# A gated linear attention with a sine-squared MLP behind it: state sums off the tensor engine, paired half blocks, and a new order of work

## The chip, the cores and the metric

The kernel runs on one core of one Trainium2 chip. The metric is the device time of one launch in microseconds; before the change the median of 11 runs is 222.42 us (220.28 to 224.2). The engines of the core work beside each other and wait for each other by semaphores: PE (TensorE, matmuls; its weight loads are shown as PEld), DVE (VectorE), ACT (ScalarE), POOL (GpSimd) and SP (SyncE), which here issues most DMAs.

## The reference, cut to what matters

```python
f = 1.0 / (1.0 + np.exp(-f_logit))                 # B, H, S, D = 4, 8, 768, 48
for t in range(S):
    state = f[:, :, t, :, None] * state + np.einsum('bhd,bhe->bhde', k[:, :, t], v[:, :, t])
    y[:, :, t] = np.einsum('bhd,bhde->bhe', q[:, :, t], state)
x = y.transpose(0, 2, 1, 3).reshape(B * S, H * D)  # 3072 tokens, 384 features
h = x @ w_in                                       # w_in is 384 x 2048
s = np.sin(alpha * h)
g = h + s * s / (alpha + 1e-09)
out = g @ w_out                                    # w_out is 2048 x 384
```

All inputs and the output are float32.

## The kernel before

The sequence is cut into six chunks of 128 steps. A chunk c has four batches b, so 512 tokens. Inputs are loaded and prepared in units u of half a chunk (two batches): u = 2c and 2c+1; a unit and batch pair has the number m. The work has these stages; the names are those of the tiles in the profile.

- **load** (line 271): 48 loads of 384 KB, four per unit (f, k, q, v), all on SP's queue in the order of the list LOADS. The MLP's weights come on POOL's queue: w_in in two halves of eight DMAs (line 295), w_out in four (line 305). Each group stands behind a one-element copy on POOL (`seen`, line 287) that waits for one of the loads; W_GATE says for which position in LOADS.
- **pre(u)**: ACT computes Exp and Ln of the gate logits (lines 333 and 336, tiles f and lf). PE forms their running sums with a triangular mask (cs, lines 363 and 366, five matmuls, and one in the last chunk). ACT takes two exponentials of each (Gi and cs, lines 376 and 372). k times Gi goes to POOL or DVE and q times cs to DVE (qk, line 385); gl (line 380) is the decay over the chunk; v is cast into vb by DVE (lines 342 and 343).
- **attend(c, b)**: q and k are transposed by PE (tp, line 420) and copied to SBUF (tr, line 428) in chunks 0 to 3, or transposed by DMA on SP in chunks 4 and 5 (line 426). Then come the score matmuls (aps, line 437), the causal mask on DVE (at, line 440), the part of the output from the old state (y, line 445, "inter") and from the chunk itself (y, line 458), and the eviction into xT (line 465).
- **the state**: except in the last chunk PE forms k^T v (kv, line 473). From chunk 1 on, one matmul of 512 columns with the identity first adds the old state into the same PSUM tile (line 471). DVE then multiplies the sum by the decay (st, line 479).
- **spread(c)**: six small DMAs on SP or POOL put the features in place in xT (line 508).
- **first(c, fb)**: the MLP's first layer for one of 16 blocks of 128 hidden features. Three matmuls make h (line 529), ACT takes the sine (s, line 534), the square is made by POOL, DVE or ACT (s2, shown as s; lines 542 and 540), and DVE adds it to h (g, line 547). The PSUM bank of h is held until g is done. h has three banks; in chunk 0 some blocks use the two banks of the second layer instead (SPARE). In chunk 0 the layer is done in halves of two batches (256 columns), one half block to a bank; later chunks take 512 columns.
- **second(c, t)**: sixteen matmuls over the g tiles (o, line 566), an eviction (osb, line 574) and a store (line 577).

Exp and Ln share one ACT table and the sine needs another, so ACT's work is cut into phases with a table load (line 628) at each change. PHASES lists them: `("pre", [6, 7, 8])` is the preparation of these units, `("sin", 18)` the next 18 sines. The sines run through the blocks of chunk 0, first half, then second half, then chunk 1 and so on.

The order of everything is found by a planner in the kernel (`in_order`), which runs when the program is built. Each operation has a duration for each engine that may do it, its inputs, the ring of buffers that it takes from, and a rank; the planner starts, again and again, the operation with the smallest start time (plus a BIAS where several engines can do it), and ranks decide ties. KIND, RANK, LAG and ATT are offsets to the ranks by kind of operation and chunk. The instructions of an engine then run strictly in the order that came out. Four lists are kept in a given order whatever the planner finds: loads, ACT's table work, h, and cs.

```python
                key = (s + (BIAS[e] if len(o.engs) > 1 else 0), o.rank, s + d)
...
            if not first:
                nc.tensor.matmul(kv, ident, tl["st", c - 1, b], start=True, stop=False, skip_group_check=True)
...
        hb, sb, s2b = buf("o" if spare else "h"), buf("s"), buf("s2")
```

Of the kernel before, what the change touches and what calls it, by code (L numbers as in the profile page):

```python
# [10 lines left out]
F32 = mybir.dt.float32  # L11
# [6 lines left out]
NG = 36  # L18
PE_TR = 4
SPARE = 15  # L20
LOADS = [("k", 0), ("f", 0), ("q", 0), ("v", 0), ("f", 1), ("v", 1), ("q", 1), ("k", 1), ("f", 3),
    ("k", 3), ("f", 2), ("q", 3), ("q", 2), ("f", 5), ("v", 3), ("v", 2), ("k", 2), ("k", 4),
    ("f", 4), ("v", 4), ("q", 4), ("k", 5), ("v", 6), ("q", 5), ("k", 7), ("v", 7), ("f", 6),
    ("v", 5), ("k", 6), ("f", 7), ("q", 6), ("v", 10), ("f", 8), ("q", 7), ("q", 8), ("k", 8),
    ("v", 8), ("k", 11), ("v", 9), ("v", 11), ("f", 11), ("f", 9), ("k", 9), ("q", 10), ("k",
    10), ("q", 9), ("q", 11), ("f", 10)]
W_GATE = [1, 6, 15]
LAG = [389, 183, 51, 210, 208, 289]
ATT = [150, -130, -181, 58, -47, 55]
PHASES = [("pre", [0]), ("pre", [1]), ("sin", 16), ("pre", [2, 3]), ("sin", 15), ("pre", [4, 5]),  # L30
    ("sin", 17), ("pre", [6, 7, 8]), ("sin", 18), ("pre", [9, 10, 11]), ("sin", 46)]
RANK = [-6, 628, -691, -10, 175, 71, 8, 20, -437, -18, -103, -123]
MULS = {"POOL": 1020, "DVE": 750}
KIND = {"v": [147, 9, 46, 75, 127, -2],
        "cs": [-145, -32, -204, -182, -55, -258],
        "kh": [-179, -112, -104, -31, -147, -299],
        "qh": [-145, -50, -132, -383, -199, -136],
        "tp": [-133, -167, -186, -203, -128, -244],
        "tr": [116, 196, 76, 293, 139, 285],
        "a": [-282, -297, -247, -321, -246, -206],  # L40
        "m": [83, 264, 119, 421, 58, 182],
        "y": [-85, 152, 24, 75, 105, 196],
        "i": [81, 10, -86, -217, 109, 54],
        "kv": [148, 97, 59, 86, 61, 178],
        "st": [129, 130, -157, 126, 215, -54],
        "h": [5, -27, 43, 31, -36, -92],
        "sq": [114, 125, 112, 12, 253, 139],
        "g": [-119, 51, -134, 78, 119, -14],
        "ev": [-69, -174, -183, -117, -240, -203]}
SPREAD = {"SP": 1800, "POOL": 1600}  # L50
BIAS = {"ACT": 400, "DVE": 500, "POOL": 500, "SP": -1800}
# [12 lines left out]
class Op:  # L64
    after, line = 0, None
# [11 lines left out]
def in_order(ops, lines):  # L77
# [28 lines left out]
    while left:  # L106
        best = None
        for o in pending:
# [5 lines left out]
            for e, dur in o.engs.items():  # L114
                s = max(t, free[e])
                if o.dma:
                    s = max(s, dma_free[e] - DMA_AHEAD)
                d = dur + (TABLE_LOAD if o.table and o.table != table and table else 0)
                key = (s + (BIAS[e] if len(o.engs) > 1 else 0), o.rank, s + d)
                if best is None or key < best[0]:  # L120
                    best = (key, o, e, s, d)
# [28 lines left out]
def kernel(  # L150
# [60 lines left out]
    def op(rank, engs, emit, deps=(), takes=(), holds=(), table=None, dma=None):  # L211
# [8 lines left out]
        h=N_H, s=3, s2=3, g=NG, o=2, osb=3).items()}  # L220
# [105 lines left out]
    def pre(u, rank):  # L326
        c = u // NU
# [24 lines left out]
        made["v", u] = op(rank + KIND["v"][c] + 2, {DVE: 1300 if u < NU else 1050}, values, deps=[vb_.ready], takes=[vv], holds=[vb_])  # L352
        late = []
        for i in range(2):
# [34 lines left out]
            c_ = op(rank + KIND["cs"][c] + i, {PE: 170 if last else 370}, cs_, deps=[l], takes=[cb], holds=[lf])  # L389
# [7 lines left out]
            made["kh", m] = op(rank + KIND["kh"][c] + i, MULS, km, deps=[gi, kb_.ready], takes=[qkb], holds=[kb_, Gib])  # L397
            made["qh", m] = op(rank + KIND["qh"][c] + i, {DVE: 490}, qm, deps=[g, qb_.ready], takes=[qkb], holds=[qb_, cb])
# [5 lines left out]
    def attend(c, b, rank):  # L404
# [4 lines left out]
        yb, kvb, sb = buf("a"), buf("a"), buf(f"st{b}")  # L409
# [58 lines left out]
        def kv_(e):  # L468
            kv = tl[x, "kv"] = ps_a.tile([P, HP, 2, E], F32, tag="a", name=f"kv_{c}_{b}")
            if not first:  # L470
                nc.tensor.matmul(kv, ident, tl["st", c - 1, b], start=True, stop=False, skip_group_check=True)
            for p in range(HP):
                nc.tensor.matmul(kv[:, p, :, :], qk_b[qkb.place % NQ][:, 0, p, :, :].rearrange("c r e -> c (r e)"),  # L473
                                 v_b[vb.place % NV][:, p, i, :, 0, :],
                                 start=(first and p == 0), stop=True, skip_group_check=True)

        def st_(e):
            t = tl["st", c, b] = st_pool.tile([P, HP, 2, E], BF16, tag=f"s{b}", name=f"st_{c}_{b}")
            nc.vector.tensor_tensor(t, tl[x, "kv"], tl["gl", m].unsqueeze(3).to_broadcast([P, HP, 2, E]),  # L479
                                    Alu.mult)  # L480

        if c < PE_TR:
            kt = op(rank + KIND["tp"][c], {PE: 250}, lambda e: tp_(e, 0), deps=[made["kh", m]], takes=[tpb], holds=[qkb])
            qt = op(rank + KIND["tp"][c], {PE: 250}, lambda e: tp_(e, 1), deps=[made["qh", m], kt], holds=[tpb, qkb])
            tr = op(rank + KIND["tr"][c], {DVE: 640, ACT: 970}, tr_, deps=[qt], takes=[trb], holds=[tpb])
        else:
            tr = op(rank, {SP: 1300}, tr_, deps=[made["kh", m], made["qh", m]], takes=[trb], holds=[qkb], dma=3000)
        a = op(rank + KIND["a"][c], {PE: 400}, a_, deps=[tr], takes=ab + atb, holds=[trb])
        ms = [op(rank + KIND["m"][c], {DVE: 640}, lambda e, r=r: m_(e, r), deps=[a], holds=[ab[r], atb[r]]) for r in range(2)]
        last_ = None  # L490
        if not first:
            last_ = op(rank + KIND["i"][c], {PE: 265}, inter_, deps=[a, made["st", c - 1, b]], takes=[yb], holds=[trb, sold])
        for r in range(2):
            last_ = op(rank + KIND["i"][c], {PE: 350 if first else 240}, lambda e, r=r: intra_(e, r), deps=[ms[r], last_, made["v", u]],
# [165 lines left out]
```

## Time and profile before

| | us |
|---|---|
| median of 11 runs | 222.42 |
| the profiled execution | 222.77 |
| its span, first to last instruction | 221.0 |
| PE busy (weight loads) | 187.4 (116.0) |
| DVE busy | 164.4 |
| ACT busy | 165.1 |
| POOL busy | 99.6 |
| mean granted PE clock | 0.959 |

The rows of the costliest groups that the change touches, with the shapes kept apart (columns: line, engine, operation, output from input with its shape, count, busy us, mean ns of one, idle time of the engine just before them and what ended it):

```profile
L534 ACT ACTIVATE s<-h,al_p 128x512 f32<-128x512 f32 x80 | 53.7, 687 | 18.0 <-PE h L529 16.4
L542 POOL TENSOR_TENSOR s<-s 128x512 f32<-128x512 f32 x45 | 46.6, 1042 | 59.0 <-ACT s L534 50.4 <-DVE at L440 3.3 <-DVE g L547 2.5
...
L479 DVE TENSOR_TENSOR st<-kv,gl 128x512 bf16<-128x512 f32 x20 | 13.3, 685 | 6.9 <-PE kv L473 6.9
...
L542 POOL TENSOR_TENSOR s<-s 128x256 f32<-128x256 f32 x20 | 12.0, 611 | 12.5 <-ACT s L534 8.6 <-DVE s L542 2.5 <-DVE g L547 1.1
...
L628 ACT ACT_TABLE_LOAD x9 | 11.5, 1283 | 0.2
...
L471 PE MATMUL kv<-st,ident 128*128 128x512 bf16 x16 | 6.1, 381 | 0.0
...
L540 ACT ACTIVATE s<-s 128x256 f32<-128x256 f32 x8 | 3.1, 418 | 0.1
L542 DVE TENSOR_TENSOR s<-s 128x256 f32<-128x256 f32 x4 | 2.2, 559 | 1.5 <-ACT s L534 1.5
```

A matmul's mean here is from its issue to its modelled end, so that consecutive ones overlap: three of 512 columns take 0.65 us together, not 3 times 0.38. Squares and sines share the name s, since numbers in names are left out.

### The profile page before, as it was taken

Reading aid. Unit: us, or ns where it says so; the run is one execution under the profiler, and the core shown is the slowest. Engines: PE = TensorE matmul, PEld = TensorE weight load, DVE = VectorE, ACT = ScalarE, POOL = GpSimd, SP = SyncE. Lnnn points to the kernel's source line nnn. Section 1 sums busy time; section 2 is a strip of 40 time slices with the busy share of each in tenths; the row PEclk is TensorE's granted clock in tenths of the full one; section 3 lists DMA queues with packets and bytes.
Section 4 is the critical chain, followed back from the end, with each engine's and each line's share of the span. In section 5 each row is a group of like instructions: output and inputs, shape, how many; then the busy total and the mean of one; then the engine's idle time right before and its main releaser. Section 6 shows DMA issues by size and latency. Waiting matters only on the chain.

```text
span 221.0 us, 4306 instructions
## 1 busy us (share of the span) xinstructions
PE 187.4 (85%) x1513; PEld 116.0 (52%) x1529; DVE 164.4 (74%) x301; ACT 165.1 (75%) x275; POOL 99.6 (45%) x134
## 2 busy tenths in 40 slices
PE   0269656596999898987799999999999999999993
PEld 0157444474776455653465655566665555555561
DVE  7667766568788999895679989567978958778700
ACT  2545946988569879799978888988877887777511
POOL 5721756059244735673733265375364642123300
PEclk9999997559999999999799999999999999999999
DMA  8999999999990999989599998464500101100211
GB/s 133 189 201 188 192 195 198 189 172 196 188 180 19 174 191 194 175 145 225 142 171 198 175 153 164 136 176 95 98 25 34 73 18 39 38 34 36 74 71 71
DMA packets 115125, 29.61 MB, mean 134 GB/s; under 512 B 108720, under 2 KB 114336, under 8 KB 115104
## 3 DMA queue, kind: packets, MB, share of 16 engines
q1 hardware_dynamic: 111648, 26.04, 67.8%
q0 software_dynamic: 3456, 3.30, 9.0%
q8 instruction: 12, 0.20, 0.4%
q14 instruction: 9, 0.07, 0.1%
HBM read 25.17 MB, written 4.72 MB: 135 GB/s over the span
## 4 chain that ended last, share of the span: by engine, by line
PE 60%; ACT 11%; DMA 10%; DVE 6%; SPq 5%; issue 4%; POOL 2%; ACTq 0%
PE o L566 25%; PE h L529 23%; SPq L271 5%; DMA q<-in_q_dram 4%; PE y L458 4%; DMA w_in_bf<-in_moe_w_in_dram 3%; DMA w_out_bf<-in_moe_w_out_dram 3%; ACT f L333 3%; DVE g L547 2%; PE aps L437 2%; PE y L445 2%; ACT Gi L376 2%; ACT L628 2%; POOL w_in_bf L295 2%; ACT s L534 2%
## 5 line engine op out<-in xcount | busy, mean ns | idle before, releaser
L542 POOL TENSOR_TENSOR s<-s 128x512 f32<-128x512 f32 (+1 forms) x65 | 58.5, 909 | 71.5 <-ACT s L534 59.0
L534 ACT ACTIVATE s<-h,al_p 128x512 f32<-128x512 f32 (+1 forms) x112 | 67.7, 627 | 27.5 <-PE h L529 25.0
L529 PE MATMUL h<-xT,w_in_bf 128*128 128x512 bf16 (+1 forms) x320 | 76.9, 356 | 7.3 <-DVE g L547 3.3
L547 DVE SCALAR_TENSOR_TENSOR g<-s,al_r,h 128x512 bf16<-128x512 f32 (+1 forms) x112 | 72.0, 667 | 12.6 <-POOL s L542 10.1
L566 PE MATMUL o<-w_out_bf,g 128*128 128x384 bf16 x384 | 78.4, 330 | 1.2 <-DMA w_out_bf<-in_moe_w_out_dram 1.2
L566 PEld LDWEIGHTS <-g 128*128 128x128 bf16 x384 | 36.5, 99 | 25.7 <-issue 2.0
L529 PEld LDWEIGHTS <-w_in_bf 128*128 128x128 bf16 x336 | 32.4, 100 | 30.1 <-issue 4.2
L440 DVE TENSOR_TENSOR at<-aps,mask 128x512 bf16<-128x512 f32 x48 | 31.5, 685 | 3.5 <-PE aps L437 3.2
L385 POOL TENSOR_TENSOR qk<-k,Gi 128x384 bf16<-128x384 f32 x22 | 21.6, 1000 | 17.9 <-ACT Gi L376 17.8
L540 ACT ACTIVATE s<-s 128x512 f32<-128x512 f32 (+1 forms) x36 | 20.8, 584 | 0.9
L385 DVE TENSOR_TENSOR qk<-q,cs 128x384 bf16<-128x384 f32 x24 | 13.2, 552 | 10.2 <-ACT cs L372 10.0
L363 PE MATMUL cs<-lf,mask 128*128 128x384 bf16 x24 | 9.0, 382 | 12.5 <-ACT lf L336 10.3
L458 PE MATMUL y<-at,vb 128*128 128x128 bf16 x184 | 18.7, 229 | 0.3 <-DVE at L440 0.3
L479 DVE TENSOR_TENSOR st<-kv,gl 128x512 bf16<-128x512 f32 x20 | 13.3, 685 | 6.9 <-PE kv L473 6.9
L420 PE MATMUL tp<-ident,qk 128*128 128x128 bf16 x128 | 12.1, 251 | 4.2 <-POOL qk L385 2.0
L333 ACT ACTIVATE f<-f 128x768 f32<-128x768 f32 x12 | 10.0, 836 | 6.1 <-POOL seen L287 5.1
L458 PEld LDWEIGHTS <-vb 128*128 128x128 bf16 x184 | 13.3, 103 | 2.4 <-issue 0.2
L574 ACT COPY osb<-o 128x384 f32<-128x384 f32 x16 | 7.6, 478 | 9.1 <-PE o L566 8.9
L437 PE MATMUL aps<-tr 64*128 64x128 bf16 x192 | 10.5, 228 | 4.5 <-DVE tr L428 3.2
L376 ACT ACTIVATE Gi<-cs 128x384 f32<-128x384 f32 x24 | 11.6, 484 | 3.4 <-PE cs L366 2.7
L420 PEld LDWEIGHTS <-qk 128*128 128x128 bf16 x128 | 9.9, 113 | 7.7 <-POOL qk L385 3.7
L465 ACT CAST xT<-y 128x512 bf16<-128x512 f32 (+1 forms) x20 | 11.2, 565 | 1.3 <-PE y L458 1.1
(56 smaller groups left out, 171.5 us busy)
## 6 DMA issues: line engine op xcount, KB each, us to landing
k<-in_k_dram SPq DMA_DIRECT2D x12, 384.0 KB, 6.7
f<-in_f_logit_dram SPq DMA_DIRECT2D x12, 384.0 KB, 6.9
q<-in_q_dram SPq DMA_DIRECT2D x12, 384.0 KB, 6.6
v<-in_v_dram SPq DMA_DIRECT2D x12, 384.0 KB, 7.1
out_dram<-osb SPq DMA_DIRECT2D x24, 192.0 KB, 1.9
w_out_bf<-in_moe_w_out_dram POOLq DMA_DIRECT2D x4, 384.0 KB, 7.8
w_in_bf<-in_moe_w_in_dram POOLq DMA_DIRECT2D x8, 128.0 KB, 5.9
w_in_bf<-in_moe_w_in_dram POOLq DMA_DIRECT2D x4, 96.0 KB, 6.6
```

The costliest lines, as they stand in the source:

```text
L333: nc.scalar.activation(out=tl["f", u], in_=tl["f", u], func=Act.Exp, scale=-1.0)
L376: nc.scalar.activation(out=tl["Gi", m], in_=tl["cs", m][:, :H * D], func=Act.Exp)
L385: engine[e].tensor_mul(qk_b[bufs["qk", m].place % NQ][:, "kq".index(n), :, :, :D], tl[n, u][:, i * H:(i + 1) * H, :].rearrange("c (r p) d ...
L420: nc.tensor.transpose(tl[x, "tp"][:, j * HP + p, :], qk_b[qkb.place % NQ][:, j, p, :, :].rearrange("c r e -> c (r e)"), ident)
L440: nc.vector.tensor_mul(tl[x, "at", r], tl[x, "a"][r], mask4)
L458: nc.tensor.matmul(tl[x, "y"][:, blk, :], v_, tl[x, "at", r][:, p, :], start=(first and p == r == 0), stop=(r == 1), skip_group_check=True)
L529: nc.tensor.matmul(h[:, :n], w_in_bf[:, kb, fs], xT[:, kb, ts], start=(kb == 0), stop=(kb == KB - 1))
L534: nc.scalar.activation(out=s[:, :n], in_=tl[x, "h"][:, :n], func=Act.Sin, scale=al_p[:, fb:fb + 1])
L540: nc.scalar.activation(out=s2[:, :n], in_=s[:, :n], func=Act.Square)
L542: engine[e].tensor_mul(s2[:, :n], s[:, :n], s[:, :n])
L547: nc.vector.scalar_tensor_tensor(tl["g", c, fb][:, ts], tl[x, "s2"][:, :n], al_r[:, fb:fb + 1], tl[x, "h"][:, :n], Alu.mult, Alu.add)
L566: nc.tensor.matmul(tl["o", c, t], tl["g", c, fb][:, t * P:(t + 1) * P], w_out_bf[:, fb, :], start=(fb == 0), stop=(fb == FB - 1))
```

## The change

- **State sums.** From chunk 2 on (SUM = 2) the identity matmul is left out. DVE adds kv and the old state into a new SBUF tile `sum` (two buffers), and the product with gl then reads `sum` and runs on POOL or DVE; in the built program all twelve run on POOL.
- **Pairs in chunk 0.** Two half blocks of 256 columns share one PSUM bank and one s tile. Their sines stay separate (each block has its own scale), the square is one operation over 512 columns, and the two additions stay separate. In the built program all 16 squares of chunk 0 run on POOL.
- **Buffers.** g has 44 buffers in place of 36. SPARE goes from 15 half blocks to 5 pairs.
- **Order.** KIND has an offset for each unit instead of each chunk, ON_ACT adds a bias for ACT by kind and unit, and LOADS, W_GATE, LAG, ATT, PHASES, RANK and BIAS have new values. In PHASES the stage of units 6, 7 and 8 becomes units 6 and 7, three sines, and unit 8.

In the built program the counts on the engines change as follows; all others stay.

| | before | after |
|---|---|---|
| PE: identity matmuls, 512 columns | 16 | 4 |
| DVE: st / sum | 20 / 0 | 8 / 12 |
| POOL: st | 0 | 12 |
| squares of 256 columns, POOL / ACT / DVE | 20 / 8 / 4 | 0 / 0 / 0 |
| squares of 512 columns, POOL / ACT / DVE | 45 / 28 / 7 | 63 / 26 / 7 |
| k products, POOL / DVE | 22 / 2 | 20 / 4 |
| evictions osb, ACT / DVE | 16 / 8 | 10 / 14 |
| copies tr, ACT / DVE | 9 / 7 | 10 / 6 |
| evictions xT, ACT / DVE | 20 / 4 | 18 / 6 |
| ACT table loads | 10 | 12 |

The diff, cut to its core:

```diff
-NG = 36
+NG = 44
-SPARE = 15
+SUM = 2
+SPARE = 5
-W_GATE = [1, 6, 15]
-PHASES = [("pre", [0]), ("pre", [1]), ("sin", 16), ("pre", [2, 3]), ("sin", 15), ("pre", [4, 5]),
-    ("sin", 17), ("pre", [6, 7, 8]), ("sin", 18), ("pre", [9, 10, 11]), ("sin", 46)]
+LOADS = [("v", 0), ("f", 0), ("q", 0), ("k", 0), ("f", 1), ("v", 1), ("q", 1), ("k", 1), ("v", 2),
+    ("f", 2), ("f", 3), ("k", 3), ("q", 2), ("q", 3), ("f", 5), ("v", 3), ("k", 2), ("q", 5),
+    ("q", 4), ("v", 4), ("f", 4), ("k", 4), ("v", 6), ("f", 6), ("k", 5), ("k", 6), ("v", 5),
...
+W_GATE = [5, 5, 18]
+PHASES = [("pre", [0]), ("pre", [1]), ("sin", 16), ("pre", [2, 3]), ("sin", 16), ("pre", [4, 5]),
+    ("sin", 13), ("pre", [6, 7]), ("sin", 3), ("pre", [8]), ("sin", 19), ("pre", [9, 10, 11]),
+    ("sin", 45)]
...
-                key = (s + (BIAS[e] if len(o.engs) > 1 else 0), o.rank, s + d)
+                key = (s + (BIAS[e] + (o.on_act if e == "ACT" else 0) if len(o.engs) > 1 else 0), o.rank, s + d)
...
         def kv_(e):
...
-            if not first:
+            if not first and c < SUM:
                 nc.tensor.matmul(kv, ident, tl["st", c - 1, b], start=True, stop=False, skip_group_check=True)
...
+        def sum_(e):
+            t = tl[x, "sum"] = at_pool.tile([P, HP, 2, E], F32, tag="sum", bufs=2, name=f"sum_{c}_{b}")
+            nc.vector.tensor_tensor(t, tl[x, "kv"], tl["st", c - 1, b], Alu.add)
...
-            nc.vector.tensor_tensor(t, tl[x, "kv"], tl["gl", m].unsqueeze(3).to_broadcast([P, HP, 2, E]),
-                                    Alu.mult)
+            engine[e].tensor_tensor(t, tl[x, "kv"] if c < SUM else tl[x, "sum"],
+                                    tl["gl", m].unsqueeze(3).to_broadcast([P, HP, 2, E]), Alu.mult)
...
+                su = op(rank + KIND["st"][u] + 1, {DVE: 640}, sum_, deps=[kv, sold_op], holds=[sumb, kvb, sold])
+                made["st", c, b] = op(rank + KIND["st"][u] + 1, {POOL: 1040, DVE: 917}, st_, deps=[su, made["gl", m]],
+                                      holds=[sb, sumb, bufs["gl", m]])
...
-    def first(c, fb, ts, rank, needs):
+    def first(c, fbs, ts, rank, needs):
...
+        part = [slice(i * n, (i + 1) * n) for i in range(len(fbs))]
+
+        def mm(e, i):
             pool_, tag = (ps_o, "o") if spare else (ps_h, "h")
...
+                nc.tensor.matmul(tl[x, "h"][:, part[i]], w_in_bf[:, kb, fbs[i] * P:(fbs[i] + 1) * P],
+                                 tl["xT", c][:, kb, ts], start=(kb == 0), stop=(kb == KB - 1))
...
+                engine[e].tensor_mul(s2, s, s)
...
-            for fb in range(FB):
-                sins.append(first(0, fb, HALF[half], 16 * half - 32 + fb, needs(half, fb)))
+            for fb in range(0, FB, 2):
+                sins += first(0, (fb, fb + 1), HALF[half], 16 * half - 32 + fb, needs(half, fb))
```

## The prediction

> **What bounds the kernel now.** I read, in this order and shown so, the page's slices, the windows by stage, the list of waits, ScalarE's timeline at its table loads, and the chain of waits.
>
> ```profile
> PE   0269656596999898987799999999999999999993
> ...
> PEclk9999997559999999999799999999999999999999
> ...
> 75.00:97.40 22.40, 20.59 (x183) 12.26 (x184) 21.32 (x36) 17.96 (x28) 11.88 (x12) 1.00 1.14 184
> 97.40:111.00 13.60, 9.83 (x78) 5.42 (x78) 8.73 (x22) 13.26 (x23) 8.05 (x10) 0.87 0.77 168
> 111.00:135.00 24.00, 23.84 (x209) 14.40 (x209) 21.51 (x36) 20.10 (x33) 10.15 (x12) 1.00 1.17 176
> 135.00:153.00 18.00, 17.89 (x144) 10.93 (x145) 12.69 (x24) 16.58 (x28) 9.79 (x10) 1.00 0.51 130
> 153.00:207.00 54.00, 53.68 (x366) 29.43 (x370) 43.06 (x63) 42.24 (x68) 20.26 (x20) 1.00 0.18 49
> ...
> ACT s L534 <- PE h L529: 25.0, 45, 2.0
> ...
> 97.44 1.28 ACT L628 ACT_TABLE_LOAD   x1
> ...
> 109.49 1.28 ACT L628 ACT_TABLE_LOAD   x1
> 110.79 1.84 ACT L534 ACTIVATE s<-h,al_p 128x512 f32<-128x512 f32 x3
> ...
> 135.59 1.28 ACT L628 ACT_TABLE_LOAD   x1
> ...
> 115.59 0.38 PE h L529
> ...
> 192.09 0.65 PE h L529 x3
> ...
> 207.00 10.41 PE o L566 x64
> ```
>
> In a window line the figures after the length are the busy us of PE, its weight loads, DVE, ACT and POOL, then clock, DMA share, GB/s. ScalarE's sines wait 25.0 us in 45 waits for h. From 111 on PE is busy throughout; before that other engines pace it (DVE 21.3 of 22.4 in chunk 1's first layer; ACT 13.3 of 13.6 in the exp stage from 97.4, where PE loses 3.8). A busy PE hides pipelining, so I count places on PE instead: 0.216 us per 512 columns (three in 0.65), 0.1625 for an o matmul (64 in 10.41), 0.056 for 128 columns (tp, eight in 0.45), 0.041 for one of the paired aps (eight in 0.33), 0.33 for a cs of five. Summed over the instruction list this is 170.9 us. PE ends at 217.4, so 46.5 us are idle or at half clock, nearly all before 115. From block 3 of chunk 2 (115.6) there are 100.9 us of places for 101.8 us. Earlier, every PE wait is repaid; later, only less PE work or a new wait counts.
>
> **What the Trainium skill says.** "TensorE: Matmul & The Clock Gate", section "Wait — 56ns, not 53.3ns?", gives 215.7 ns and 55.6 ns for 512 and 128 columns on a warm array; the trace agrees (0.216, 0.056). Its section "What's actually happening" halves the clock after an idle window: here the granted clock was 0.50 from 40 to 48 us. "ScalarE: Activation LUTs", section "What ACT_TABLE_LOAD costs", gives 1283 ns and a further drain of some 1380. The trace has 1283, and the next activation 0.02 us later, so I use 1.3. "SBUF — State Buffer", section "Who interferes with whom", says that a DVE operation with one SBUF input does not contend with GpSimd, one with two does. The new sum reads one SBUF and one PSUM operand, so it should run like st (684 ns); the casts of v do get blocked (one took 2.72 us at 72.36).
>
> **The change part by part.** The built program's order says what stands where.
>
> 1. Identity matmuls: 12 of 16 go (chunks 2 to 4), 12 × 0.216 = 2.6 us of PE; total 168.3.
>
> 2. The states of these chunks: each st on DVE (0.685) becomes a sum on DVE, taken at 0.685, and a product on POOL, taken at the square's 1.04 since shape and operands are alike (bounds 0.7 and 1.5, as the trace has no broadcast factor on POOL). DVE +0, POOL +12.5. The state is ready some 1.3 us later (1.04 and a hand-over of about 0.2). Behind it stand the next chunk's inter matmuls, which follow after 18 us of PE places or more, so I charge nothing; without that cover each would stall PE by up to 1.3. On POOL the squares and k products queued behind wait up to 1.04; POOL is busy 45%.
>
> 3. Pairs in chunk 0: 32 half squares become 16 full ones. All go to POOL: 16 × 1.04 = 16.7 for 20 × 0.61 before, and 8 × 0.42 = 3.3 us leave ACT, 4 × 0.56 = 2.2 DVE. With two half blocks per bank, six rather than two of the second half's blocks run on PE during the exp stage that starts at 37.9.
>
> 4. Weights and loads: both halves of w_in now follow the sixth load. SP's issues go by about 2.05 us apart and the seventh load landed at 21.2 with 4.3 us of w_in ahead of it, so the sixth lands near 15. The second half of before took 10.1 us from first issue (21.47) to use (31.58); so the first half lands near 25.4 instead of before 21.5, and 16 issues hold POOL for 8.2 us. One tr also moves ahead of the table load. The first sine starts near 28.4 (24.5 before). But before ScalarE then waited twice for h, 2.0 and 1.9 us, the first for w_in's second half; I let both vanish. w_out follows the nineteenth load and POOL's squares, issued about 56 to 63 instead of 48.3 to 54.2; o starts only near 62, so I charge nothing; a landing after 68 would hold cs and cost 1 us per us. On SP the first transpose of chunk 4 now stands ahead of nine loads: nine × 2.05 = 18.5 us after about 111, for first use near 136; free unless 5 us late.
>
> 5. ACT's path. To the first Exp of the stage at 64.9, ACT work falls from 43.9 to 40.7 us (same unit durations for both); with fewer waits I put the first sine of chunk 1 at 71.1, 3.7 earlier than 74.9. Block 0 to block 12: PE places 17.9 instead of 16.5, so 18.1 us becomes 19.5; the sine of block 12 ends at 91.2 (93.5 before). From there to the end of chunk 2's first sine ACT has 21.0 us instead of 16.7: pre of units 6 to 8 is split around three sines, which adds two table loads (2.6), squares and evictions. With the 1.2 us of waits seen before: 91.2 + 22.2 = 113.4 (111.4 before).
>
> 6. Block 3 of chunk 2 needs the bank of block 0: square 1.04, g 0.74, hand-overs 0.3: 115.5, as good as before (115.6). But behind that point stand 94.9 us of PE work instead of 100.9: 1.3 from identity matmuls, 4.7 from output matmuls and others now done in the split stage. That is the gain: 6.0.
>
> 7. What is late next: the last exp stage (units 9 to 11). It now opens after chunk 3's block 2 (before: after block 1, at 135.59, with the next sine at 149.19). Block 6 needs the bank of block 3, so the stage, then sine 3, square and g: 16.5 us after block 2 (0.9 to the table load, 13.0 for the stage without the eviction in it, 0.65, 1.15, 0.8). Between the two PE has 12.9 us of work; before, from block 1 to block 5, it had 17 us of places for 17.6 us. PE starves 3.6 us.
>
> 8. Chunk 4: all 16 squares on POOL, 16 × 1.04 = 16.7 for 21.1 us of PE; a bank turns in about 3.7 us, three banks give 1.23 per block against PE's 1.32. Free, with little to spare: at 4.4 us per turn, 0.15 × 16 = 2.4 us.
>
> Sum: 115.5 + 18.9 (to the end of block 2) + 0.3 + 16.5 + 63.1 + 0.6 = 214.9, and the last eviction and store 3.6: span 218.5 against 221.0. The profiled execution took 222.77, 1.77 more than its span; so 220.3, and as it lies 0.35 above the median of the runs, 219.9.
>
> **The rivals.**
>
> Larger gain: the front gains more, or the starved stage finds PE behind, so the 3.6 of step 7 vanish. For it: 46.5 us of slack to win. Against it: the pacing there is ACT's, in order. 219.9 − 3.6 = 216.3.
>
> No gain: step 6's gain is given back, 3.6 in step 7 and 2.4 in step 8. −6.0 + 6.0 leaves 222.4. For it: POOL's square of one block is the longest link; against: POOL idles 33.7 of 54 us from 153 to 207.
>
> Slower: the front comes later instead of earlier because w_in is late. Place: the first sine of chunk 0. The end follows the sine of block 12 one for one: 219.9 + (t − 91.2). If the 3.9 us of late start are made up only by half, t is 95.5 and the time 224.2. It is slower by over 0.5% from t = 94.8. For it: ACT's path from there is 4.3 us longer, and two table loads cannot be hidden once ACT paces; against: 3.3 us of squares leave ACT.
>
> That the sums do not shorten PE can't be: the 12 matmuls are gone from the list; but their worth is only the 1.3 to 2.6 of step 1.
>
> **How the numbers follow.** Forecast 0.42, larger gain 0.22, no gain 0.14, slower 0.22. A measurement here tells 0.5% (1.1 us) from no change. So faster 0.64, same 0.14, slower 0.22. The likeliest alone spans 217.5 to 221.3. Steps 7 and 8 at their worst with the late front reach 225.5; the larger gain with the front earlier by a further 2.5 reaches 213.8.
>
> **What would show it.** Right: chunk 1's first sine near 71, chunk 2's first table load to sine at 113, block 3 of chunk 2 near 115.5, an idle PE of 3 to 4 us inside the last exp stage, POOL products near 1.04, sums near 0.685. Wrong: the first sine of chunk 0 after 29, cs waiting for w_out, h waiting for POOL's squares in chunk 4, or loads of unit 9 landing after the last exp stage opens.

## The result and the profile after

| | before | after |
|---|---|---|
| median of the runs, us | 222.81 (47 runs, the first 11 among them, 220.11 to 225.47) | 225.89 (12 runs, 224.04 to 227.29) |
| ratio after / before | | 1.0171, 95% interval 1.0136 to 1.0206 |
| profiled execution, us | 222.77 | 224.48 |
| its span, us | 221.0 | 222.7 |
| sine of block 12 of chunk 1 ends | 93.5 | 91.4 |
| h of block 3 of chunk 2 starts on PE | 115.6 | 119.08 |
| PE goes on with chunk 3 in the last exponential stage | no gap | 154.86 |

The change costs 1.7% by the ratio; the medians differ by 3.1 us, which is 1.4%. Some executions of a kernel run at a lower granted clock and take longer: the ratios, here and below, leave these slow ones out, the medians don't. The profiled execution of after shows only 1.7 us of the 3.1, because it lies 1.4 us under its own median while that of before lies on its median. The twelve runs list their granted clock: at 0.946 to 0.953 they took 225.75 to 227.29 us, at 0.961 and above 224.04 to 224.95, and the profiled one had 0.969.

The same views of the kernel after: two rows of the page's slices, then the windows by stage (sines of chunk 1; exponentials of chunk 3; sines of chunk 2; last exponentials; the rest), with busy us of PE, its weight loads, DVE, ACT, POOL, then clock, DMA share, GB/s.

```profile
PE   0269692859988999969698999988999999999993
...
PEclk9999999785999999969999999999999999999999
```

```profile
71.75:91.95 20.20, 19.63 (x190) 12.42 (x192) 18.30 (x28) 16.56 (x25) 14.17 (x14) 1.00 1.21 183
91.95:115.15 23.20, 19.08 (x166) 11.54 (x166) 19.10 (x36) 19.97 (x31) 12.05 (x14) 0.93 0.95 186
115.15:139.30 24.15, 23.10 (x173) 12.92 (x174) 21.96 (x33) 19.43 (x32) 12.71 (x14) 1.00 0.97 156
139.30:154.85 15.55, 13.63 (x108) 7.53 (x107) 11.76 (x24) 15.24 (x25) 12.33 (x13) 1.00 0.72 166
154.85:207.00 52.15, 51.30 (x346) 28.39 (x353) 41.20 (x61) 36.47 (x58) 27.20 (x28) 1.00 0.15 43
```

The front is earlier: chunk 1's sines start at 71.76 instead of 74.9, and PE is busy 19.6 of 20.2 us there. The loss is in the second and fourth line. In the second no engine is full: 19 to 20 of 23.2 us on PE, DVE and ACT each, so the three wait for each other. The granted clock is 0.93 there, a point taken up below. ScalarE's waits for h as a whole (us, times, longest) have shrunk from 25.0 in 45 to:

```profile
ACT s L555 <- PE h L549: 21.7, 39, 1.6
```

In the fourth window PE is idle for about 2 us (busy PE hides pipelining; by places the gap is larger) while ACT is busy throughout.

ScalarE's table loads and the sines that open chunk 2, from its timeline:

```profile
91.96 1.28 ACT L660 ACT_TABLE_LOAD   x1
...
102.79 1.28 ACT L660 ACT_TABLE_LOAD   x1
...
106.98 1.28 ACT L660 ACT_TABLE_LOAD   x1
...
113.85 1.28 ACT L660 ACT_TABLE_LOAD   x1
115.14 1.85 ACT L555 ACTIVATE s<-h,al_p 128x512 f32<-128x512 f32 x3
...
119.98 0.69 ACT L555 ACTIVATE s<-h,al_p 128x512 f32<-128x512 f32 x1 [1.56 <-PE h L549]
```

From the load at 91.96 to that at 113.85 it takes 21.89 us. What held it is in the chain of waits (start, us, engine, tile and line; the chain that ended last, so each piece released the next):

```profile
94.05 2.20 DVE vb L347
...
96.52 0.48 DVE osb L605
...
105.38 1.32 DVE s L564
106.70 0.60 DVE at L445
...
116.99 0.91 ACT tr L433
117.94 0.38 PE aps L442 x7
...
149.75 2.27 POOL qk L390 x2
152.02 0.51 POOL st L488
...
152.99 1.04 POOL s L564
154.06 0.76 DVE g L570
```

A cast of v takes 2.20 us on this chain. Its reason is seen by putting DVE's timeline beside POOL's and PE's:

```profile
93.97 2.28 DVE L347 CAST vb<-v 128x384 bf16<-128x384 f32 x1
96.17 0.35 DVE L348 CAST vb<-v 128x384 bf16<-128x384 f32 x1
96.44 0.55 DVE L605 COPY osb<-o 128x384 f32<-128x384 f32 x1
```

```profile
93.97 2.05 POOL L488 TENSOR_TENSOR st<-sum,gl 128x512 bf16<-128x512 f32 x2
```

```profile
97.04 2.40 PE L597 MATMUL o<-w_out_bf,g 128*128 128x384 bf16 x7 [1.35 <-DVE osb L605]
...
107.36 0.38 PE L463 MATMUL y<-at,vb 128*128 128x128 bf16 x4 [1.56 <-DVE at L445]
```

Two state products start on POOL at 93.97, the cast starts beside them and ends 0.2 us after them; the next cast of the same size takes 0.35. Behind the cast stands the eviction of an output bank, behind that an output matmul on PE, behind that the running sums cs, and ScalarE waits 1.50 us for those at 99.88. The same happens at 105.38, where a square on DVE takes 1.32 us beside two more products, and the mask that PE waits 1.56 us for stands behind it.

Not all of the 1.50 us is waiting for the eviction. The seven output matmuls behind it take 2.40 us, where seven places of 0.1625 are 1.14, because PE runs at half clock just then. A window of after shows it (clock 0.50), and PE's timeline of x_nosum (below; no state products on POOL) shows the same seven at full clock:

```profile
98.00:100.00 2.00, 2.00 (x12) 0.99 (x11) 0.77 (x4) 0.50 (x2) 0.99 (x2) 0.50 0.26 94
```

```profile
96.36 1.30 PE L600 MATMUL o<-w_out_bf,g 128*128 128x384 bf16 x7
```

So some 1.1 us (2.40 less 1.30) of what ScalarE waits for is the lower clock. The profiles go together: in after, x_tr33, x_sq4 and a_defer PE waits 1.34 or 1.35 us for this eviction, and in one of the windows of 2 us after it the clock is between 0.50 and 0.58; in x_cast, x_all3, x_nosum, n_v7 and n_v7b the wait is gone and the clock stays at 1.00 from 90 to 108 us. That the wait brings the drop is the likely reading; no run here changes the one without the other.

### The profile page after: what moved, and what is told of

Its sections match the earlier page's. It is cut to its first block, busy times and chain, and to the rows that moved or that the text cites. A ratio compares the mean times of both kernels' runs of the same rounds, so it can differ in the third digit from the quotient of the medians.

```text
span 222.7 us, 4241 instructions
## 1 busy us (share of the span) xinstructions
PE 187.0 (84%) x1501; PEld 115.5 (52%) x1517; DVE 171.5 (77%) x306; ACT 161.1 (72%) x260; POOL 117.4 (53%) x142
## 3 DMA queue, kind: packets, MB, share of 16 engines
q1 hardware_dynamic: 111648, 26.04, 67.4%
## 4 chain that ended last, share of the span: by engine, by line
PE 55%; ACT 14%; DVE 11%; DMA 9%; POOL 4%; SPq 3%; issue 2%; ACTq 0%; POOLq 0%
PE h L549 25%; PE o L597 21%; ACT s L555 4%; SPq L277 3%; PE y L463 3%; DMA w_out_bf<-in_moe_w_out_dram 3%; DMA v<-in_v_dram 3%; DVE g L570 3%; ACT L660 3%; DMA w_in_bf<-in_moe_w_in_dram 3%; DVE vb L347 2%; DVE vb L348 2%; PE aps L442 2%; ACT f L338 2%; ACT cs L377 2%
## 5 line engine op out<-in xcount | busy, mean ns | idle before, releaser
L564 POOL TENSOR_TENSOR s<-s 128x512 f32<-128x512 f32 x63 | 65.6, 1051 | 46.0 <-ACT s L555 37.5
L555 ACT ACTIVATE s<-h,al_p 128x512 f32<-128x512 f32 (+1 forms) x112 | 66.3, 629 | 24.4 <-PE h L549 21.7
L549 PE MATMUL h<-xT,w_in_bf 128*128 128x512 bf16 (+1 forms) x320 | 78.0, 364 | 4.7 <-DMA w_in_bf<-in_moe_w_in_dram 2.2
L597 PE MATMUL o<-w_out_bf,g 128*128 128x384 bf16 x384 | 77.0, 330 | 2.6 <-DVE osb L605 1.4
L549 PEld LDWEIGHTS <-w_in_bf 128*128 128x128 bf16 x336 | 33.4, 103 | 27.9 <-DMA w_in_bf<-in_moe_w_in_dram 3.0
L390 POOL TENSOR_TENSOR qk<-k,Gi 128x384 bf16<-128x384 f32 x20 | 20.5, 1042 | 23.0 <-DMA k<-in_k_dram 8.4
L488 POOL TENSOR_TENSOR st<-sum,gl 128x512 bf16<-128x512 f32 x12 | 12.4, 1044 | 10.4 <-DVE sum L484 10.3
L562 ACT ACTIVATE s<-s 128x512 f32<-128x512 f32 x26 | 16.3, 632 | 0.5
L470 ACT CAST xT<-y 128x512 bf16<-128x512 f32 (+1 forms) x18 | 10.4, 583 | 6.5 <-PE y L463 5.4
L433 ACT COPY tr<-tp 128x1024 bf16<-128x1024 bf16 x10 | 10.1, 1012 | 6.6 <-PE tp L425 6.6
```

The lines of the kernel that those rows point to most:

```text
L390: engine[e].tensor_mul(qk_b[bufs["qk", m].place % NQ][:, "kq".index(n), :, :, :D], tl[n, u][:, i * H:(i + 1) * H, :].rearrange("c (r p) d ...
L549: nc.tensor.matmul(tl[x, "h"][:, part[i]], w_in_bf[:, kb, fbs[i] * P:(fbs[i] + 1) * P], tl["xT", c][:, kb, ts], start=(kb == 0), stop=(kb ...
L555: nc.scalar.activation(out=tl[x, "s"][:, part[i]], in_=tl[x, "h"][:, part[i]], func=Act.Sin, scale=al_p[:, fbs[i]:fbs[i] + 1])
L562: nc.scalar.activation(out=s2, in_=s, func=Act.Square)
L564: engine[e].tensor_mul(s2, s, s)
L597: nc.tensor.matmul(tl["o", c, t], tl["g", c, fb][:, t * P:(t + 1) * P], w_out_bf[:, fb, :], start=(fb == 0), stop=(fb == FB - 1))
```

## The experiments

All keep the order that the planner gave (of after, unless it says before) and move single operations in it; `move` puts an operation before or after another one on its queue. The kernel before was timed beside each of them, with medians between 222.5 and 223.1, and each ratio is against it. A difference of two ratios counts as clear below when it is larger than both intervals together allow (the root of the sum of their squared half widths); of the runs that keep the order of after, x_nosum and n_v7b are clear of it on the faster side. The diffs are shortened to what they do. The line numbers of these kernels lie a few lines higher.

**Three local waits (theory A), the load of the sums (B), the table loads (C).**

x_cast, x_tr33, x_all3:

```diff
+move(cast of v_10, after=sum_3_1)                    # x_cast, x_all3
+move(tr_3_3, after=tr_3_2, engine=DVE)               # x_tr33, x_all3
+move(both masks of at_3_0, before=square s2_1_14)    # x_all3
```

> The changed kernel with its order kept, except that the cast of v of unit 10 on DVE (needed only in the last chunk) stands after the sums of chunk 3 instead of ahead of the eviction of o_0_2. Theory A (three local waits between 91 and 119 us make block 3 of chunk 2 late; the first is this cast, held 2.2 us by two state products on POOL, then the eviction, o_1_0, cs_14 and ScalarE's Gi_14 behind it): the wait of 1.35 us of o for DVE and the 1.5 us of Gi for PE go, chunk 2's first sine starts 1.3 to 2.0 us earlier than 115.1, time 1.2 to 2.0 us under the changed kernel's 225.9. Theory B (the sums themselves load DVE and POOL too much): 0 to 0.5 us. Theory C (the two added table loads alone lengthen ScalarE's path): the wait goes but another takes its place, 0 to 0.5 us.

> The changed kernel with its order kept, except that the copy tr_3_3 runs on DVE right after tr_3_2 instead of on ScalarE behind a table load and three sines. Theory A: the 0.75 us wait of aps for ScalarE goes and block 3 of chunk 2 starts 0.7 to 1.0 us earlier than 119.1, time 0.6 to 1.0 us less than the changed kernel. Theory C: PE then waits for the bank of block 0 instead, under 0.3 us. Theory B: no change.

> Both moves, and the two masks at_3_0 ahead of the square of block 14 of chunk 1 on DVE. Theory A: block 3 of chunk 2 starts 3.0 to 3.6 us earlier than 119.1, time 222.5 (3.0 to 3.6 us under the changed kernel). Theory C: 0 to 1 us in all. Theory B: at most 1.5 us.

Measured: x_cast 224.95 (ratio 1.0126, 1.0062 to 1.019), x_tr33 225.41 (1.0139, 1.008 to 1.0198), x_all3 224.74 (1.0121, 1.0063 to 1.018). None of the three is clear of after (0.5%, 0.3% and 0.5% less, each within 0.7%). Moving the cast shortened the stretch from the table load to the one at chunk 2's sines from 21.89 to 20.73 us, a little less than the 1.3 to 2.0 us of A and about as much as the lower clock had cost. But x_all3, with all three, needs 21.31, and from the first table load to block 3 of chunk 2 it takes 25.93 us in place of 27.12: 1.2 us less, where A asked for 3.0 to 3.6. First DVE's timeline, then PE's, show why:

```profile
103.82 0.55 DVE L347 CAST vb<-v 128x384 bf16<-128x384 f32 x1
104.29 1.20 DVE L348 CAST vb<-v 128x384 bf16<-128x384 f32 x1
105.40 0.68 DVE L433 COPY tr<-tp 128x1024 bf16<-128x1024 bf16 x1
```

```profile
106.13 0.38 PE L450 MATMUL y<-tr,st 128*128 128x128 bf16 x4 [1.73 <-DVE tr L433]
```

The moved cast now stands beside the next two products (POOL, 103.11 to 105.27), takes 1.75 us in its two parts, and holds a copy that PE waits 1.73 us for. One wait went, another of the same kind came.

x_nosum (identity matmuls back, no sums, states on DVE as before the change):

```diff
-sum_c_b on DVE, st_c_b = sum * gl on POOL            # c = 2, 3, 4
+identity matmul into kv, st_c_b = kv * gl on DVE
```

> The changed kernel with its order kept, with the identity matmul back in chunks 2 to 4 and the product on DVE in the place of the sum; nothing of the states on POOL. Theory A: PE gets 2.6 us of places back, of which 1.3 lie behind block 3 of chunk 2, and the cast before the eviction of o_0_2 is no longer held by POOL (2.28 us back to 0.35), so 1.5 us come back in the split stage: the time lies within 1 us of the changed kernel. Theory B: 2 us or more faster. If the sums paid off as a whole: 1.3 to 2.6 us slower.

Measured: 224.23 (1.0104, 1.0065 to 1.0144). So the state part isn't worth the 1.3 to 2.6 us of the matmuls it saves; with it the kernel is at 1.0171, without it at 1.0104: it costs 0.7%, about 1.5 us. The two intervals just overlap; the difference is 0.67% and uncertain by 0.53%. The stretch of the exponentials is 19.50 us here, 2.4 less, with the clock at 1.00 throughout. To block 3 of chunk 2 only 1.0 us of that is left (26.11 from the table load, for 27.12), because another wait follows, shown under theory D.

b_sum and b_sumdve do the reverse: the kernel before with its own order, and the state part alone. In b_sum the products are on POOL, in b_sumdve on DVE right behind the sums.

```diff
-if not first: identity matmul
+if not first and c < 2: identity matmul
...
+sum = kv + st (DVE); st = sum * gl (POOL in b_sum, DVE in b_sumdve)    # c >= 2
```

> The kernel before with its order kept; only the state part of the change is made: in chunks 2 to 4 no identity matmul, a sum on VectorE in place of the state product there, and the state product on POOL behind it. The forecast's step 1 (12 identity matmuls are 2.6 us of a PE that sets the pace in at least half of that time) asks for 1.3 to 2.6 us less than before: 220.2 to 221.5. Theory B (the sums load VectorE and POOL too much: POOL's products hold VectorE's casts) asks for no gain or a loss: 222.8 to 224.5.

> b_sum (before's order; no identity matmul, a sum on VectorE, 228.9) with the state products of chunks 2 to 4 on VectorE, right behind the sums, instead of on POOL. If b_sum lost its 5.9 us in POOL's queue (the products stand there ahead of the spread of chunk 2 and of the squares of chunk 2's end), most of it comes back: 222.5 to 224.5. If VectorE's own load is what counts, it stays at 227 or more, since VectorE now has 12 x 0.685 us more.

Measured: b_sum 228.93 (1.0272, 1.0224 to 1.032), b_sumdve 224.75 (1.0081, 1.0045 to 1.0116). POOL's queue is what b_sum pays for. POOL's timeline, then PE's:

```profile
96.91 1.04 POOL L483 TENSOR_TENSOR st<-sum,gl 128x512 bf16<-128x512 f32 x1 [1.46 <-DVE sum L482]
97.90 1.60 POOL L512 DMA_DIRECT2D xT<-xT  x3
...
136.63 1.04 POOL L483 TENSOR_TENSOR st<-sum,gl 128x512 bf16<-128x512 f32 x1 [2.21 <-DVE sum L482]
137.63 1.04 POOL L546 TENSOR_TENSOR s<-s 128x512 f32<-128x512 f32 x1
138.63 1.04 POOL L483 TENSOR_TENSOR st<-sum,gl 128x512 bf16<-128x512 f32 x1
```

```profile
102.71 1.01 PE L533 MATMUL h<-xT,w_in_bf 128*128 128x512 bf16 x2 [2.59 <-DMA xT<-xT]
...
139.51 0.81 PE L533 MATMUL h<-xT,w_in_bf 128*128 128x512 bf16 x3 [1.24 <-DVE g L551]
```

A product that waits 1.46 us for its sum stands ahead of the spread of chunk 2, and PE waits for that. Near 137 products and squares take turns on POOL, 1.04 us each, and PE waits for g. The casts aren't what b_sum loses by: together they take 14.7 us, for 13.8 before. With the products on DVE 1.9 of the 2.7% come back. What stays, 0.8% above before with 12 matmuls less on PE, is most likely DVE's own added time (12 products of 0.73 us); no run takes it alone.

x_stdve asks the same in the order of after:

```diff
+move(st_c_b, after=sum_c_b, engine=DVE)              # c = 2, 3, 4
```

> The changed kernel with its order kept; the state products of chunks 2 to 4 go from POOL to VectorE, right behind their sums, so nothing of the state is on POOL and no product can hold a cast, but VectorE has 8.2 us more. If POOL's products (blocked casts, POOL's queue) are the whole cost of the sums, as fast as x_nosum or faster: 223 to 224.2. If VectorE's own time counts as much, 225.5 to 226.5.

Measured: 226.94 (1.0205, 1.0141 to 1.0269), 1.0% above x_nosum, which is clear, and not to be told from after. DVE's added time (12 products of 0.77 us, 9.3 us) costs about as much as POOL's products did; in chunk 2's stage DVE is busy 23.9 of 25.0 us. Theory B holds for both engines: neither has room for these products where they fall.

x_two takes two of the added table loads out by moving three sines with their squares and g:

```diff
+move(sines, squares, g of blocks 13, 14, 15 of chunk 1, after=h of block 15)
+move(first Exp of unit 6, after=those)
```

> The changed kernel with its order kept, but blocks 13 to 15 of chunk 1 (sines, squares, g) moved ahead of the exponentials of chunk 3, so that all three units of that exponential stage follow each other and two of ScalarE's table loads (2 x 1.28 us) go. The third unit's gates were issued at 99.4 and are likely there only near 106, so ScalarE may wait for them, and the first sine of chunk 2 should start at 111.7 to 113.0 instead of 115.1. Theory C (the two added loads lengthen ScalarE's path): 2 to 3.4 us faster than the 225.9 of the changed kernel, 222.5 to 223.9. Theory A (only the waits behind the cast, the masks and the transpose copy count): the loads are covered by these waits, 225 to 226.

Measured: 227.53 (1.0237, 1.0181 to 1.0293), slower still. ScalarE waits 3.96 us for the gates f_8, and PE stands 4.90 us at the cs matmuls, since its own order was made for the split stage. So C isn't supported, and isn't cleanly refuted either: the loads can't be had out by moving ScalarE's work alone. x_best combined it with x_nosum:

```diff
+x_nosum + x_two
+move(tr_3_3, after=tr_3_2, engine=DVE)
+move(square of block 3 of chunk 3, before=masks of at_4_1, engine=DVE)
```

> The changed kernel with the identity matmuls back and no sums (as in x_nosum, 224.2), blocks 13 to 15 of chunk 1 ahead of the exponentials (as in x_two), the copy tr_3_3 on VectorE, and in chunk 3 the square of block 3 on VectorE ahead of the masks of chunk 4. If ScalarE's path from the sine of block 12 to block 3 of chunk 2 is what counts, all three add up: 1 to 3 us less than x_nosum, 221.2 to 223.2, and at the low end below the kernel before. If something else follows close behind (PE's own work, or loads that come late), 223.5 to 224.5.

Measured: 229.48 (1.0295, 1.0252 to 1.0338), 1.9% above x_nosum: the moved sines again cost more than the two loads save, and PE again stands 4.90 us at the cs matmuls.

x_sq4 tests step 8 of the prediction, that all of chunk 4's squares on POOL are free:

```diff
+squares of blocks 1, 4, 7, 10, 13 of chunk 4: POOL -> ACT
```

> The changed kernel with its order kept; in chunk 4 five of the sixteen squares (blocks 1, 4, 7, 10, 13) go from POOL to ScalarE. Step 8 of the forecast says that all squares of chunk 4 on POOL cost nothing: within 0.5 us of 225.9. If POOL's squares held g back there, at least 1 us faster; if ScalarE's time counted there, at least 1 us slower.

Measured: 226.45 (1.0104, 1.004 to 1.0168). The ratio is 0.67% below that of after, uncertain by 0.73%, so by the times alone a gain of 1 us isn't out. The traces settle it: the order of both kernels is the same up to block 6 of chunk 3, and from there to the end it takes 67.84 us in after and 67.85 in x_sq4. Step 8 stands.

**Late loads (theory D).** In x_nosum, with the products gone, the stretch ended on another wait. DVE's timeline, then PE's:

```profile
113.23 1.06 DVE L347 CAST vb<-v 128x384 bf16<-128x384 f32 x1 [1.22 <-DMA v<-in_v_dram]
114.21 1.15 DVE L348 CAST vb<-v 128x384 bf16<-128x384 f32 x1
...
115.35 0.54 DVE L390 TENSOR_TENSOR qk<-q,cs 128x384 bf16<-128x384 f32 x1
```

```profile
116.04 0.61 PE L425 MATMUL tp<-ident,qk 128*128 128x128 bf16 x8 [2.06 <-DVE qk L390]
```

The load of v_7 lands at 113.2, its cast is slow again (k products run on POOL), and a q product stands behind it. x_sp, n_sp and n_sp3 bring loads forward in SP's queue; n_sp_two adds x_two's move.

```diff
+move(loads k_4, v_6, f_6, k_5, v_5, q_6, before=spread of chunk 1)    # x_sp, n_sp, n_sp_two
+move(loads f_8, k_8, k_7, v_8, v_7, before=spread of chunk 2)         # x_sp, n_sp, n_sp_two
+move(loads k_7, v_7, before=spread of chunk 2)                        # n_sp3
+x_nosum, and tr_3_3 on DVE                                            # n_sp, n_sp3, n_sp_two
```

> The changed kernel, arithmetic and engines untouched; only SP's queue is put in another order: six loads (k_4, v_6, f_6, k_5, v_5, q_6) stand ahead of the spread of chunk 1, behind which the queue stood still from 50 to 66.5, and five (f_8, k_8, k_7, v_8, v_7) ahead of the spread of chunk 2. Theory D (loads held back in SP's queue are what ends the stretch before chunk 2, or follow close behind the local waits): products and casts of the unit 7 no longer wait for k_7 (landed at 110.2) and v_7 (113). If D is the main cause, at least 2 us faster than 225.9: 222 to 224. If the local waits of theory A (cast, masks, transpose copy) stand in front of it, 225 to 226.

> x_nosum (identity matmuls back, no sums, 224.2) with SP's queue put in the order of x_sp and the copy tr_3_3 on VectorE. There the local waits are gone already, and the trace shows the load of v_7 landing at 113.2, its cast behind it, and PE waiting 2.06 us for the q product behind that cast. Theory D: this goes, 1.5 to 2.5 us less than x_nosum: 221.7 to 222.7, as fast as before. If ScalarE's own work is the bound there, 223.7 to 224.5.

> x_nosum (224.2) with only the loads k_7 and v_7 moved in SP's queue, ahead of the spread of chunk 2, and the copy tr_3_3 on VectorE; the queue up to there is as in the changed kernel, so w_out and the spread of chunk 1 aren't delayed as in n_sp (226.7). n_sp ran from the table load after chunk 2's stage begins to the next in 24.85 us, x_nosum in 27.06. Theory D in that stretch: 1.5 to 2.2 us less than x_nosum, 222.0 to 222.7. If the moved loads delay the spread of chunk 2 or the gates f_8, 223.5 to 225.

> n_sp with blocks 13 to 15 of chunk 1 ahead of the exponentials as in x_two, so two table loads less. x_two waited 3.96 us for the gates f_8 and then for v_7; with both loaded early the two table loads (2.56 us) should come out of ScalarE's path. Theories C and D together: 1 to 2.5 us less than n_sp, near 220 to 221.5. If moving the three blocks costs PE or VectorE more than the loads save (the sine of block 15 ended 3.7 us later in x_two, not 3.0), 222.5 to 224.5.

Measured: x_sp 229.04 (1.0319, 1.0281 to 1.0357), n_sp 226.69 (1.0192, 1.015 to 1.0234), n_sp3 227.73 (1.0217, 1.0173 to 1.0262), n_sp_two 231.35 (1.0409, 1.0363 to 1.0455). The stretch that the loads were meant for did shrink: chunk 2's sines, from their table load to the next, took 24.85 us in n_sp and n_sp3, 27.06 in x_nosum. But other transfers paid: n_sp comes to the first table load 4.6 us later than x_nosum (97.33 for 92.77), and in n_sp3 the exponentials take 25.29 us for 19.50. First PE in x_sp, then ScalarE in n_sp3:

```profile
67.31 1.46 PE L601 MATMUL o<-w_out_bf,g 128*128 128x384 bf16 x8 [1.15 <-DMA w_out_bf<-in_moe_w_out_dram]
...
75.49 0.39 PE L551 MATMUL h<-xT,w_in_bf 128*128 128x512 bf16 x1 [1.29 <-DMA xT<-xT]
```

```profile
104.29 0.48 ACT L610 COPY osb<-o 128x384 f32<-128x384 f32 x1 [4.08 <-DMA out_dram<-osb]
```

The six loads ahead of chunk 1's spread delay w_out (PE waits for it 2.8 us in four places, 1.1 us in one in after) and the spread itself; the two ahead of chunk 2's spread delay the stores behind it, so that an eviction on ScalarE waits 4.08 us for its buffer. D as a cause of the loss is out (in x_sp the stretch of the exponentials is 22.04 us, as in after). As the next bound behind A and B it is right.

n_v7 and n_v7b take the same wait away on DVE instead, without touching transfers:

```diff
+x_nosum
+move(tr_3_3, after=tr_3_2, engine=DVE)
+move(cast of v_7, after=tr_3_3)                      # n_v7
+move(cast of v_7, after=g of block 2 of chunk 2)     # n_v7b
```

> x_nosum (224.2) with SP's queue untouched: the copy tr_3_3 goes to VectorE behind tr_3_2, and the cast of v_7 behind both, so that the q product and the copies of chunk 3 no longer stand behind a cast whose load lands at 113.2. In x_nosum PE waited 2.06 us there. Theory D in its narrow form (one late load at the head of VectorE's queue): block 3 of chunk 2 comes 1.5 to 2 us earlier than in x_nosum, 222.2 to 222.8, as fast as before. If another wait takes its place once more, 223.7 to 224.5.

> As n_v7, but the cast of v_7 stands behind g of block 2 of chunk 2 on VectorE. In n_v7 the cast took 2.15 us there (POOL's k products were running beside it) and stood ahead of the xT copy and of g of block 0, so block 3 of chunk 2 waited 2.17 us for g in place of 2.06 us for the q product. Behind g of block 2 nothing that block 3 needs stands behind the cast. If that wait is what ends the stretch, block 3 comes near 116.5 instead of 118.7 and the whole 1.5 to 2.2 us below x_nosum: 222.0 to 222.7. If the stretch's end is set by something else by now, 223.7 to 224.9.

Measured: n_v7 224.87 (1.0124, 1.0061 to 1.0186), n_v7b 223.58 (1.0038, 1.0013 to 1.0064; 22 runs). In n_v7 the cast took 2.15 us and held g of block 0, so PE waited 2.17 us for that. In n_v7b it is behind everything that block 3 needs. PE's timeline of n_v7b:

```profile
116.96 0.81 PE L551 MATMUL h<-xT,w_in_bf 128*128 128x512 bf16 x3 [0.29 <-DVE g L572]
...
120.85 0.38 PE L450 MATMUL y<-tr,st 128*128 128x128 bf16 x4 [1.03 <-DVE at L445]
```

Block 3 starts at 116.96, 24.55 us after the end of the sine of block 12 at 92.41; the forecast had 24.3 between the same two points (91.2 to 115.5). Half of the gain is lost again 4 us later, at 120.85, to a mask behind the moved cast. It is the best version found: 1.3% faster than after by the ratios (1.0% by the medians, 223.58 for 225.89), but still 0.4% slower than before. No version here beats the kernel before.

**The starved last exponential stage.** a_defer and n_all move PE work into it:

```diff
+move(matmuls 2 to 15 of block o_2_1, before=o_2_2)   # a_defer, n_all
+n_sp3                                                # n_all
```

> The changed kernel with its order kept; 14 of the 16 matmuls of block o_2_1 (2.3 us of PE) go out of chunk 2's stage, where PE is busy 18.8 of 19 us, into the last exponential stage, where PE starves (15.1 of 17 busy). Step 7 of the forecast put that starving at 3.6 us. If PE alone sets the pace of chunk 2's stage, the exponentials start up to 2.3 us earlier and the whole with them: 223.6 to 224.5. If VectorE, busy 17.75 of 19 there, follows close behind, less than 1 us: 225 to 225.9.

> n_sp3 with the 14 matmuls of o_2_1 moved as in a_defer. With VectorE unloaded of the sums (16.4 of 19 us busy in x_nosum), PE sets the pace of chunk 2's stage, so the move should give 1 to 2.3 us below n_sp3: 220 to 221.5, less than the kernel before. If it gives nothing here either, the pace of that stage is ScalarE's or VectorE's: 222 to 223.

Measured: a_defer 226.44 (1.0158, 1.0102 to 1.0214), n_all 227.72 (1.0228, 1.0183 to 1.0273). With 2.3 us of PE work gone from chunk 2's sines their stage shrank by only 0.45 us in a_defer (25.45 to 25.00) and 0.66 in n_all against n_sp3: PE now waits for g from DVE (in a_defer 0.21 us at 137.00, and 0.63 us just behind the stage), and DVE is busy as long as before, 23.1 us for 23.3. And the exponential stage became longer, as PE waits for evictions of the moved block (0.43 us at 149.68 in a_defer). The 3.6 us aren't to be had this way.

## Why the prediction was wrong

The profiled execution came out 4.2 us above the forecast of 220.3 (224.48), and the median 1.4 us above the profiled execution where the forecast had put it 0.35 below. Of the 4.2, 3.6 lie before block 3 of chunk 2 (119.08 for 115.5), 0.6 behind it.

- **Step 1** was right in PE's places but not in their worth: x_nosum, with the matmuls back, isn't slower.
- **Step 2 failed**, at "so I charge nothing". The durations were right: products 1.044 us, sums 0.685, on DVE unhindered by POOL as "SBUF — State Buffer", section "Who interferes with whom", led one to expect of an operation with one SBUF input. But that rule of the section is for operations outside the two-port modes, in which VectorE also takes the ports that it shares with GpSimd. The section goes on that casts can enter these modes, and that the later of the two engines is then blocked for the other's whole instruction. The trace agrees in kind (2.28 us for a cast that takes 0.35 alone). The prediction named one blocked cast of 2.72 us, but looked only for who waits for the new state (nobody soon), not for who stands behind the DVE operations that 12.5 us of new POOL work would hold. The casts took 13.8 us together before and 18.6 after; 15.8 in x_nosum, so 2.8 of the 4.8 us more belong to the state products. The queue on POOL, up to 1.04 us a product, was named and charged nothing too; in the order of before it is what b_sum pays for. x_nosum and b_sum put the state part with its products on POOL at 0.7% in the order of after and at 2.7% in that of before: a cost, where the sum had +1.3 to +2.6 us of gain.
- **Step 3** was right in kind: squares in pairs, 16 fewer instructions in total on the three engines; no run takes it alone.
- **Step 4** was too careful: the first sine of chunk 0 came at 25.65 rather than 28.4. One of the signs of being wrong came true in small: PE waited 1.07 us for w_out until 67.4, with cs matmuls behind it, though the forecast held a landing before 68 to be harmless; ScalarE lost 0.23 us by it (at 69.44).
- **Step 5 failed** in its second half. First sine of chunk 1 71.76 (71.1), sine of block 12 ends at 91.39 (91.2): right. But "with the 1.2 us of waits seen before" took the waits of another order. ScalarE waited 1.50, 0.48, 0.54 and 0.17 us, together 2.7, all behind the blocked cast with the half clock after it, or behind the mask; chunk 2's first sine ended at 115.8 instead of 113.4. Of these 2.4 us, 1.5 are the waits, 0.2 the later start, and 0.7 work and gaps of ScalarE that the 21.0 us left out.
- **Step 6** missed one link: a transpose copy on ScalarE (tr_3_3, at 116.87, behind the table load and three sines) that PE's score matmuls wait for 0.75 us ahead of block 3. With that link and the output matmuls behind it block 3 came another 1.2 us later, 3.6 in all. Behind it the forecast held, the saved PE work and the starved stage of step 7 taken together: from there to PE's next start at 154.86 it took 35.78 us, against 35.7.
- **Step 7** was right: block 6 of chunk 3 came 16.4 us after block 2 ended (138.50 to 154.86), against 16.5, and the chain through 149.75 to 154.86 shows its last links: POOL's k products, a state product, a square, g. PE has some 13 us of places in that time, an estimate by the places per matmul of the prediction, so about 3.4 of the 6.0 us were given back, for 3.6 in the forecast.
- **Step 8** was right (x_sq4).
- **Profile against median**: the 1.8 us left of the miss. In the profiles of the ten experiments with the front of after, the table load near 92 us comes at 92.7 to 93.4 in eight (91.96 in the profiled execution of after), and the clock from 24 to 50 us was 0.80 to 0.87 in all ten (0.91 there). The clock of the exponentials varies too: x_tr33, whose mean clock is 0.947, falls to half twice there (98 to 100 and 108 to 110), and takes 23.60 us for the stretch that takes 21.89 in after and 21.96 in x_sq4, though its order up to there is the same. The one profiled execution of after was a good one.

How much of the miss is the state part? By the forecast's own terms the kernel without the sums should take 221.2 us (219.9, and the 1.3 that step 6 took off for them). x_nosum took 224.2. So about half of the 6.0 us between the forecast and the median of after goes with the sums, and 3.0 us stay without them.

Of the rivals "slower" came out in size, but not in its mechanism: the front wasn't late. What stays open is what the rest of the change costs by its parts. Without the sums it is still 1.0% slower than before. n_v7b takes 0.7% of that away by moving one late cast and the copy beside it, which shows where the time went but not which part of the change put it there; the two table loads, the pairs and the new load order weren't isolated.

## What to carry to other kernels

Work moved to GpSimd had three prices here: its own time (1.04 us a product), its place in GpSimd's queue (in b_sum a spread and squares stood behind it), and what it blocked on VectorE (casts and a square); the last one was paid by whatever stood behind the blocked instruction, not by the consumer of the new result. A wait on PE seems to cost more than its length: after 1.35 us of it the next seven matmuls took 1.1 us more at half clock. In a stretch where three engines were each idle some 15% of the time, a local repair tended to uncover a wait of like size (x_all3, n_v7, n_sp3), so a saving on one engine should be priced by a run with the rest of the order re-planned, or not counted. And a wait count taken over from the old order isn't an estimate for the new one.

## What the runs showed of the hardware

- A cast of 128x384 on VectorE that starts together with two back-to-back products of 1.04 us on GpSimd ended 0.2 us after the second, not between them: 2.28 us instead of 0.35.
- A square on VectorE with two SBUF inputs took 1.32 us beside such products, 0.68 beside none (x_all3, 107.20); the sum with one input in PSUM kept its 0.685.
- Seven output matmuls took 2.40 us in after, at a granted clock of 0.68 from 96 to 98 us and 0.50 from 98 to 100, and 1.30 us in x_nosum, at 1.00.
- Where work stood ready behind a table load of 1.28 us, the next activation began within 0.02 us (113.85 plus 1.28 is 115.13; the sine starts at 115.14). The further drain that "ScalarE: Activation LUTs", section "What ACT_TABLE_LOAD costs", gives doesn't show there.
